# Fifteen 128-wide products in place of eighteen in the second feed-forward matmul of five of eight blocks (RWKV-6 attention, then a tanh-shrink feed-forward)

## The chip, the core and the metric

The kernel runs on one core of one Trainium2 chip. A core has TensorE (PE; its weight loads are listed apart as PEld), VectorE (DVE), ScalarE (ACT), GpSimd (POOL) and SyncE (SP, which here only issues DMAs). The metric is the device time of one execution in microseconds, as the median over runs. A profiled execution gives its own time, its span (first to last instruction) and a trace of every instruction.

## The reference

All values are 32-bit floats. Attention runs over 4 batches, 8 heads, 768 tokens and a head size of 48, and its output becomes the 3072 x 384 input of a feed-forward block of width 2048.

```python
# attention: batch 4, heads 8, seq 768, head_dim 48; w in 0.80 to 0.95
for t in range(S):
    cur = einsum('bhd,bhe->bhde', u[None] * kt, vt)
    y[:, :, t] = einsum('bhd,bhde->bhe', rt, state + cur)
    state = wt[:, :, :, None] * state + einsum('bhd,bhe->bhde', kt, vt)
x = y.transpose(0, 2, 1, 3).reshape(3072, 384)
# feed-forward: w_in 384 x 2048, w_out 2048 x 384
h = x @ w_in
g = h - tanh(h)
out = g @ w_out
```

## The kernel before

The 3072 tokens are cut into 8 blocks of 384 (4 batches, two halves each). For each block the attention result is brought into three tiles `xT` of 128 x 384 (features x tokens). The feed-forward part of a block is a loop over 16 steps `f`, one for every 128 of the 2048 hidden features. In a step, PE makes `hp`, the 128 x 384 tile of `h`, with three matmuls (`first`, L629); ACT copies it to `h` with a scale (L632); `slight` gives `g`, which for the small `h` of this data is a polynomial: DVE makes `s = h*h` and records its largest value in `top` (L643), ACT makes `qa = (s + c)^2` (L645), and DVE makes `hs = h*TOP*s` and `gT = (qa + REST)*hs` (both L635). Four steps later (`LAG`) `Second.add` multiplies it with the weights: three matmuls (L676), one for each 128 tokens, with a 128 x 128 part of `gT` as the loaded operand and 384 columns of `w_out` as the moving one, accumulated over the 16 steps into three banks of PSUM. After the last step ACT copies each bank to `o` (L681) and SP stores it.

A matmul of 32-bit floats is two records of PE and two of PEld in the trace: three matmuls show as "x6".

The attention of block i+1 is made during the steps of block i. `plan(i)` says at which step which part of it is issued: DVE and ACT preparations (`before`, `ahead`), DMA loads (`loads`) and the phases of PE: `turn` (12 transposes, L386, copied out by ACT, L388), `own` and `earlier` (two products of scores each, L363, copied under a mask by DVE, L370), `update` (L405, then eleven or so short DVE steps L417 and L428 from state to state) and `result 1` and `result 2` (L469, L486, copied out by ACT, L519, with small DMAs that fill gaps in `xT`). All phases pass through a pool of two PSUM buffers (`scratch`, the tile `att`). Each of these is written and then read in the same step. The order of work on PE, ACT, DVE and SP is that in which the code issues it; each engine works through its list in that order and waits where an operand is not there. In a step of the main loop DVE's list is: `s` of this step, `hs` and `gT` of the step before, then what `plan` asks for.

In block 0 the weights are still being loaded and converted (L205 to L213, ACT and DVE). Block 7 has no attention beside it. After the last step a sum over recorded values decides whether the whole is done again in a general way (`anew`); with this data it is not.

The change touches `slight`, `Second`, `plan`, `phase`, `update_1`, `update_2`, `before`, `inverse`, and the main loop from L798.

Of the kernel before, what the change touches and what calls it, by code (L numbers as in the profile page):

```python
# [73 lines left out]
LAG = 4  # L74
# [14 lines left out]
LEAST = 2.0 ** -24  # L89

# [6 lines left out]
def kernel(  # L97
# [16 lines left out]
    gpool = ctx.enter_context(tc.tile_pool(name="gpool", bufs=LAG + 1))  # L114
    dense = ctx.enter_context(tc.tile_pool(name="dense", bufs=3))
    conv = ctx.enter_context(tc.tile_pool(name="conv", bufs=RAWS))

    shift = const.tile([P, 5], F32, name="shift", tag="shift")
    for i, value in enumerate((QUAD[0][0], QUAD[1][0], -SMALL, -1.0, SHIFT)):
        nc.vector.memset(shift[:, i:i + 1], value)  # L120
# [7 lines left out]
    seed = const.tile([P, WIDE], BF16, name="seed", tag="seed")  # L128
# [4 lines left out]
    start = const.tile([P, WIDE], F32, name="start", tag="start")  # L133
# [49 lines left out]

    blocks_n = B * NQ
    n_whole, n_excess, n_top = blocks_n * NPAIR * NCH, 2 * blocks_n, blocks_n * NF
    holds = const.tile([P, n_whole + n_excess + n_top], F32, name="holds", tag="holds")
    excess = const.tile([P, n_excess], F32, name="excess", tag="excess")
# [34 lines left out]
    class Block:  # L224
# [7 lines left out]
        def __init__(self, b, q):  # L232
            self.b, self.q = b, q
            self.cols = slice(q * NB, (q + 1) * NB)
            self.tiles = {}
            self.ks = {}
            self.kv = {}
            self.tots = {}
# [48 lines left out]
        def before(self, p0, n):  # L287
            cols = slice(p0 * NCH * LP, (p0 + n) * NCH * LP)
            return nc.vector.tensor_tensor_scan(out=self.tile("pre")[:, cols], data0=self.tile("w")[:, cols],  # L289
                                                data1=start[:, cols], initial=0.0, op0=ALU.mult, op1=ALU.add)  # L290

        def behind(self, p0, n):
# [4 lines left out]
            def back(x):  # L297
# [4 lines left out]
                data1=back(seed[:, a:a + width]), initial=1.0, op0=ALU.mult, op1=ALU.max)  # L302
# [15 lines left out]
        def inverse(self, p0, n):  # L318
            t = self.half("post", p0, n * NCH * LP).rearrange("d (c j) -> d c j", j=LP)[:, :, 1]
            tot = self.whole(p0, n)  # L320
            nc.vector.tensor_single_scalar(tot, t, LEAST, op=ALU.max)
            to = start[:, p0 * NCH * LP:(p0 + n) * NCH * LP].rearrange("d (c j) -> d c j", j=LP)[:, :, 0]
            nc.vector.reciprocal(out=to, in_=tot)
# [57 lines left out]
        def turn(self, ps, p0):  # L381
            ks = work.tile([P, UP, NCP, P], F32, name="ks", tag="ks")
# [6 lines left out]
            self.ks[p0] = ks  # L389

        def update_1(self, ps):
            last = self.q == NQ - 1
            for cs in ((0, 1), (2,)):
                kvp = self.kv[cs[0]] = scratch(ps)
                for p in reversed(range(NPAIR)):
                    ks = self.ks[p // UP * UP]
                    for c in cs:
                        for h in range(2):
                            for par in range(2):
                                if last and 2 * c + par == NCH - 1:  # L400
# [5 lines left out]
                                                 lhsT=ks[toks, p % UP, c, 64 * h:64 * h + 64],  # L406
                                                 rhs=self.v[toks, c, e0:e0 + D], start=True, stop=True)

        def update_2(self):
# [11 lines left out]
            for c in range(NCH - 1 if self.q == NQ - 1 else NCH):  # L421
                dst = St[:, :, c + 1, 0:D] if c + 1 < NCH else states[self.q + 1][:, :, 0, 0:D]
                n0 = c // 2 % 2 * NPAIR * D
                kv = self.kv[c // 4 * 2][:, c % 2, n0:n0 + NPAIR * D].rearrange("d (p e) -> d p e", e=D)
# [7 lines left out]
        def update_any(self, ps, p0, tot):  # L432
            ks, last = self.ks[p0], self.q == NQ - 1
# [76 lines left out]
        def result_out(self, pairs, apart=False, engines=None):  # L510
            copies = []
            for p in reversed(pairs):
# [4 lines left out]
                for rows in (slice(0, D), slice(64, 64 + D)) if apart else (slice(0, P),):  # L517
                    copy = engines[len(copies) % len(engines)] if engines else nc.scalar.copy
                    copies.append(copy(out=dst[rows], in_=src[rows]))  # L519
# [9 lines left out]
        def phase(self, ps, name):  # L529
            if name == "own":  # L530
                for p0 in HALVES:
                    self.own(ps, p0)()
            elif name == "earlier":
                for p0 in HALVES:
                    self.earlier(ps, p0)()
            elif name == "turn":
                for p0 in HALVES:
                    self.turn(ps, p0)
            elif name == "update":
                self.update_1(ps)  # L540
                self.update_2()
# [3 lines left out]
            elif name == "result 2":  # L545
                self.result("from_scores", ALL, True)
                self.result_out(ALL)
                self.fill_holes([nc.sync])

# [364 lines left out]
```

## Time and profile before

| what | value |
|---|---|
| median of 4 runs | 613.83 us (613.27 to 615.51) |
| profiled execution, its own time | 613.58 us |
| its span | 611.8 us |
| mean granted clock of TensorE | 0.991 |
| first step of block 0 begins at | 28.20 us |
| first step of block 1, of block 2 | 103.74 us, 175.85 us |
| each of blocks 1 to 6, first step to first step | 72.10 us |
| block 7, 16 steps without attention | 61.9 us (3.87 us a step) |
| last matmul of `hp` ends, last `o` copied | 596.5 us, 607.6 us |

The beginnings of steps are those of the first matmul on L629. "Busy" on PE counts the time in which at least one record is open; a record of 128 x 384 lasts 486 ns and the next one starts 322 ns after it, so the duration of a record is not what it costs in a row of them. The time of one more is the distance between starts.

### The profile page before, as it was taken

What the parts mean: (1) busy time and instruction counts of PE and PEld (TensorE: products, weight loads), DVE (VectorE), ACT (ScalarE), POOL (GpSimd) and SP (SyncE); (2) the same over time, 40 slices, a digit from 0 to 9 for tenths busy, and PEclk for the clock granted to TensorE, in tenths of its full rate; (3) what the DMA queues carried; (4) which work ended last, traced back from release to release, by engine and by line L of the source; (5) the groups of instructions that cost most, each with busy time, mean ns of one, the idle gap of its engine ahead of it and who ended that gap; (6) DMA issues with size and microseconds to landing.
All of it is one profiled execution on the core that took longest, in us unless ns stands there. A gap on an engine that the chain in (4) does not pass through costs nothing.

```text
span 611.8 us, 12671 instructions
## 1 busy us (share of the span) xinstructions
PE 583.8 (95%) x5410; PEld 361.1 (59%) x5410; DVE 378.1 (62%) x777; ACT 237.4 (39%) x444; POOL 11.4 (2%) x39
## 2 busy tenths in 40 slices
PE   3669899999999999999999999999999999999996
PEld 2536566666656665566655666566665666555553
DVE  8898996855376645766367563776447663444442
ACT  4879773423325322243323333252232532223222
POOL 6000000000000000000000000000000000000000
PEclk9789999999999999999999999999999999999999
DMA  8485442203202032111211122020321100001001
GB/s 329 160 338 190 159 156 64 76 3 106 63 1 78 2 106 61 40 40 53 64 52 39 41 86 83 0 78 2 105 62 40 40 2 5 8 0 39 1 0 42
DMA packets 23420, 43.03 MB, mean 70 GB/s; under 512 B 2112, under 2 KB 21312, under 8 KB 23360
## 3 DMA queue, kind: packets, MB, share of 16 engines
q1 hardware_dynamic: 22944, 41.89, 20.5%
q8 instruction: 43, 0.70, 0.5%
q10 hardware_dynamic: 352, 0.25, 0.1%
q14 instruction: 17, 0.14, 0.1%
q0 software_dynamic: 64, 0.05, 0.0%
HBM read 36.28 MB, written 4.72 MB: 67 GB/s over the span
## 4 chain that ended last, share of the span: by engine, by line
PE 88%; DVE 6%; ACT 3%; POOL 1%; issue 1%; ACTq 0%; DVEq 0%; POOLq 0%
PE acc L676 39%; PE hp L629 38%; PE att L363 3%; PE att L469 2%; PE att L405 2%; PE att L486 2%; PE att L386 1%; DVE w_sb L213 1%; POOL mask_all L144 1%; DVE post L300 1%; DVE scores L370 1%; DVE pre L289 1%; DVE gT L635 1%; DVE w_sb L212 1%; DVE s L643 0%
## 5 line engine op out<-in xcount | busy, mean ns | idle before, releaser
L629 PE MATMUL hp<-xT,w_sb 128*128 128x384 f32 x768 | 272.7, 492 | 7.1 <-DVE w_sb L213 3.0
L676 PE MATMUL acc<-w_sb,gT 128*128 128x384 f32 x768 | 271.1, 490 | 0.8
L629 PEld LDWEIGHTS hp<-xT,w_sb 128*128 128x128 f32 x768 | 145.9, 191 | 110.9 <-ACT h L632 5.9
L676 PEld LDWEIGHTS acc<-w_sb,gT 128*128 128x128 f32 x768 | 143.0, 190 | 95.3 <-issue 1.7
L643 DVE CUSTOM_DVE_ANT_0 s<-h 128x384 f32<-128x384 f32 x128 | 71.2, 556 | 196.4 <-ACT h L632 196.2
L632 ACT ACTIVATE h<-hp 128x384 f32<-128x384 f32 x128 | 62.8, 490 | 323.1 <-PE hp L629 323.1
L635 DVE SCALAR_TENSOR_TENSOR gT<-qa,hs 128x384 f32<-128x384 f32 x128 | 71.4, 558 | 16.7 <-PE acc L676 0.5
L645 ACT ACTIVATE qa<-s,shift 128x384 f32<-128x384 f32 x128 | 77.7, 607 | 0.1
L635 DVE SCALAR_TENSOR_TENSOR hs<-h,s 128x384 f32<-128x384 f32 x128 | 70.8, 553 | 0.0
L370 DVE COPY_PREDICATED scores<-mask_all,att 128x768 f32<-128x768 uint8 x32 | 30.6, 1004 | 0.1
L300 DVE TENSOR_TENSOR_SCAN post<-w,seed 128x780 f32<-128x780 f32 x16 | 28.5, 1781 | 0.0
L289 DVE TENSOR_TENSOR_SCAN pre<-w,start 128x780 f32<-128x780 f32 x16 | 28.5, 1779 | 0.0
L386 PE MATMUL att<-ident,post 128*128 128x128 f32 x96 | 12.7, 283 | 10.1 <-DVE post L314 10.1
L328 ACT ACTIVATE k<-k,u_sb 128x384 f32<-128x384 f32 x32 | 17.7, 602 | 7.2 <-DVE post L314 7.2
L386 PEld LDWEIGHTS att<-ident,post 128*128 128x128 f32 x96 | 11.4, 146 | 12.4 <-DVE post L314 10.1
L208 ACT ACTIVATE up<-raw 128x768 f16<-128x768 f32 x16 | 17.0, 1065 | 0.0
L209 ACT ACTIVATE up<-raw 128x768 uint16<-128x768 uint32 x16 | 16.8, 1051 | 0.0
L213 DVE CUSTOM_DVE_ANT_0 w_sb<-w_sb,up 128x1536 uint16<-128x1536 uint16 (+1 forms) x17 | 15.5, 911 | 1.3 <-DVE w_sb L212 0.6
L405 PEld LDWEIGHTS att<-v_sb,ks 64*64 64x64 f32 x704 | 12.0, 135 | 6.8 <-DVE scores L370 3.6
L519 ACT COPY late<-att 128x384 f32<-128x384 f32 (+1 forms) x9 | 4.3, 478 | 29.6 <-PE att L486 28.4
L405 PE MATMUL att<-v_sb,ks 64*64 64x48 f32 x704 | 13.1, 220 | 2.7 <-DVE scores L370 2.7
L428 DVE TENSOR_TENSOR states<-states,att 128x192 f32<-128x192 f32 x40 | 14.1, 354 | 2.2
(52 smaller groups left out, 260.8 us busy)
## 6 DMA issues: line engine op xcount, KB each, us to landing
raw<-in_weights SPq DMA_DIRECT2D x16, 768.0 KB, 5.0
w<-in_wT SPq DMA_DIRECT2D x7, 780.0 KB, 4.9
k<-in_kT SPq DMA_DIRECT2D x7, 768.0 KB, 4.4
r<-in_rT SPq DMA_DIRECT2D x7, 768.0 KB, 4.7
v_sb<-in_v SPq DMA_DIRECT2D x8, 576.0 KB, 3.9
out_y<-o SPq DMA_DIRECT2D x23, 192.0 KB, 2.0
xT<-late SPq DMA_DIRECT2D x44, 24.0 KB, 1.9
w<-in_wT SPq DMA_DIRECT2D x2, 390.0 KB, 5.2
```

The lines of the kernel that those rows point to most:

```text
L213: lambda: nc.vector.tensor_tensor(out=a[:, at], in0=a[:, at], in1=up[:, at], op=ALU.add)]
L289: return nc.vector.tensor_tensor_scan(out=self.tile("pre")[:, cols], data0=self.tile("w")[:, cols], data1=start[:, cols], initial=0.0, op0 ...
L300: return nc.vector.tensor_tensor_scan(out=back(t[:, 0:width]), data0=back(self.tile("w")[:, a:a + width]), data1=back(seed[:, a:a + width] ...
L370: return lambda: nc.vector.copy_predicated(out=A[:, :, p0:p0 + UP].rearrange("s h p c t -> s h (p c) t"), mask=mask.to_broadcast([P, 2, UP ...
L386: nc.tensor.transpose(tp[:, p, c * P:(c + 1) * P], self.chunk("post", p0 + p, 2 * c, n=2), ident)
L405: nc.tensor.matmul(kvp[64 * h:64 * h + 64, par, n0:n0 + D], lhsT=ks[toks, p % UP, c, 64 * h:64 * h + 64], rhs=self.v[toks, c, e0:e0 + D], ...
L629: nc.tensor.matmul(hp, lhsT=w_in_sb[:, f, kc, :], rhs=xT[kc], start=(kc == KC - 1), stop=(kc == 0))
L632: return h, nc.scalar.activation(out=h, in_=hp, func=AF.Copy, scale=1.0 / UPSCALE)
L635: return lambda: nc.vector.scalar_tensor_tensor(out=out, in0=in0, scalar=scalar, in1=in1, op0=op0, op1=ALU.mult)
L643: nc.vector.tensor_tensor_reduce(out=s, in0=h, in1=h, scale=1.0, scalar=0.0, op0=ALU.mult, op1=ALU.max, accum_out=top[:, n:n + 1])
L645: return g, [lambda: nc.scalar.activation(out=qa, in_=s, func=AF.Square, bias=shift[:, 4:5]), product(hs, h, TOP, s, ALU.mult), product(g, ...
L676: nc.tensor.matmul(acc, lhsT=g[:, j * P:(j + 1) * P], rhs=w_out_sb[:, f, :], start=(f == 0), stop=(f == NF - 1))
```

## The change

In blocks 2 to 6 (`fast`) the steps are taken in pairs. A pair holds two 128-feature tiles of `g` for three groups of 128 tokens (six 128 x 128 parts, "0a" to "2b"), and two by three 128 x 128 parts of `w_out` ("a0" to "b2"). Their 3 x 2 by 2 x 3 product takes 18 products of 128 x 128 parts; before, these were six matmuls with 384 columns each. The change uses a bilinear scheme with 15: ten sums and differences of parts of `g` (`G_FORMS`), ten of parts of `w_out` (`W_FORMS`), fifteen products of one by one, each a matmul with 128 columns, and after the block 12 instructions that put the 15 accumulated tiles together (`SUMS`).

- PE: 15 matmuls of 128 columns for each pair, in place of 6 of 384. Twelve go into the three accumulation banks, six at `now + 2` and six at `now + 3`, counted from the pair's odd step; the other three go through a `scratch` buffer, for four pairs at a time: at step 9 (pairs 0 to 3), and at steps 0 (pairs 4 to 6) and 1 (pair 7) of the next block.
- DVE: five instructions of 128 x 256 for each pair make the forms of `g`: one after the even step, four after the odd one. `s` is no longer made on DVE in these blocks. The forms of `w_out` are made once, in steps 4 to 13 of block 1, by 20 instructions of 128 x 512. The 12 `SUMS` run at steps 4 and 5 of the next block, one instruction more (`others_summed`) before them.
- ACT, in these blocks: `s = Square(h)`, `qa`, and a `Relu(s - SLIGHT)` whose accumulated sum goes to `excess`, in this order straight after `h`; before, only `h` and `qa`. At the end four copies out of PSUM (`out`).
- `h` is multiplied in place (`hs` goes away) and has three buffers for four; `LAG` is 3 for 4.
- `plan`: block 0 `turn` 4, `own` 7, `update` 9, `earlier` 11, `result 1` 13; the others `own` 4, `earlier` 6, `turn` 8, `update` 10, `result 1` 12. `own`, `earlier` and `update` hand their DVE part back, and it is issued in the following step behind `gT` (`behind`). One of the two scans of `before`, and the reciprocals, move too.
- The end: the check is summed earlier, and the last tile of rows is copied out in halves by ACT and DVE.

```diff
-LAG = 4
+LAG = 3
+PRODUCTS = ((4, 0), (5, 2), (6, 7), (7, 8), (8, "a2"), (9, 9), (2, 3), (3, 5), ("0a", "a0"),
+            ("2a", "a1"), (0, 4), (1, 6), ("0b", "b0"), ("1b", 1), ("2b", "b1"))
+AHEAD_N, MAIN = 6, 12
+    sums = const.tile([P, 16, P], F32, name="sums", tag="sums")
+    def g_at(q, x):
+        if not isinstance(x, str):
+            return 6 + q % 2 * 4 + x if x < 4 else 10 + x
+        return (q % 2 * 3 if x[1] == "a" else 20 + q % 4 * 3) + int(x[0])
+    fast = range(2, blocks_n - 1)
...
-    def slight(h, n):
+    def slight(h, n, i, f):
...
+        if i in fast:
+            at = 2 * blocks_n + fast.index(i) * NF + f
+            q, j = divmod(f, 2)
+            g = G[:, g_at(q, "0" + "ab"[j]):g_at(q, "2" + "ab"[j]) + 1].rearrange("p t c -> p (t c)")
+            nc.scalar.activation(out=s, in_=h, func=AF.Square)
+            nc.scalar.activation(out=qa, in_=s, func=AF.Square, bias=shift[:, 4:5])
+            junk = work.tile([P, UP * NCH * LP], BF16, name="junk", tag="junk", bufs=1)
+            nc.scalar.activation(out=junk[:, 0:NB], in_=s, func=AF.Relu, bias=shift[:, 5:6],
+                                 accum_out=excess[:, at:at + 1])
...
+        return g, first + [product(h, h, TOP, s, ALU.mult), product(g, qa, REST, h, ALU.add)]
+    def form_g(q, n):
+        op, (a0, b0), (a1, b1) = G_FORMS[n][0], G_FORMS[n][1:], G_FORMS[n + 1][1:]
+        to = g_at(q, n)
+        return lambda: nc.vector.tensor_tensor(out=G[:, to:to + 2], in0=two(G, g_at(q, a0), g_at(q, a1)),
+                                               in1=two(G, g_at(q, b0), g_at(q, b1)), op=OPS[op])
+    class Fewer:
+        def product(self, to, q, n, start, stop):
+            a, b = PRODUCTS[n]
...
+            nc.tensor.matmul(to, lhsT=G[:, g_at(q, a), :], rhs=rhs, start=start, stop=stop, skip_group_check=True)
+        def add(self, q, part):
+            end = q == NF // 2 - 1
+            for n in (range(AHEAD_N), range(AHEAD_N, MAIN))[part]:
+                self.product(self.acc[:, n // 4, n % 4 * P:(n % 4 + 1) * P], q, n, q == 0 and n % 4 == 0, end)
+            if end:
+                for bank in ((0,), (1, 2))[part]:
+                    self.out(4 * bank, 4, self.acc[:, bank])
+        def others(self, ps, qs):
+            if qs[0] % 4 == 0:
+                self.apart = scratch(ps)[:, 0]
...
+        def sum(self, n, m):
+            for op, *each in SUMS[n:m]:
...
+                nc.vector.tensor_tensor(out=at[0], in0=at[1], in1=at[2], op=OPS[op])
     def plan(i):
-        ahead = {13: ("behind 2", "inverse 2"), 14: ("behind 0", "inverse 0")}
+        ahead = {13: ("behind 2", "take_whole 2"), 14: ("behind 0", "take_whole 0"), 15: ("before 2",)}
...
-            phases = {5: "turn", 8: "own", 9: "update", 11: "earlier", 13: "result 1"}
+            phases = {4: "turn", 7: "own", 9: "update", 11: "earlier", 13: "result 1"}
...
-            phases = {4: "turn", 5: "own", 6: "update", 8: "earlier", 10: "result 1"}
-            before = {0: ("before 2",), 1: ("before 0",), 2: ("times_behind 2", "times_behind 0"),
-                      3: ("times_before", "held", "times_u 2"), 4: ("times_u 0",), 7: ("bound 2", "bound 0")}
+            phases = {4: "own", 6: "earlier", 8: "turn", 10: "update", 12: "result 1"}
+            before = {0: ("before 0",), 1: ("times_behind 2",), 2: ("times_behind 0", "times_u 2"),
+                      3: ("times_before", "held", "times_u 0"), 7: ("bound 2", "bound 0")}
...
         for f in range(NF):
+            now = i * NF + f
             h, made = first(here, f, ps_d)
-            g, later_ops = slight(h, i * NF + f)
-            for op in rest + extra:
+            g, later_ops = slight(h, now, i, f)
+            for op in rest + behind + extra:
                 op()
-            rest = later_ops
+            rest, behind = later_ops, []
...
+            if i in fast:
+                q = f // 2
+                rest += [form_g(q, n) for n in (range(2, len(G_FORMS), 2) if f % 2 else (0,))]
+                if f % 2:
+                    due += [(now + 2, second.add, (q, 0)), (now + 3, second.add, (q, 1))]
+                if f == 9:
+                    second.others(ps_a, range(4))
+            else:
+                due.append((now + LAG, second.add, (f, g)))
...
+            if i == 1 and fast and 4 <= f < 14:
+                for q in (0, 4):
+                    form_w(f - 4, q)
+            if f in (4, 5) and summed:
+                summed[0].sum(*((0, 6) if f == 4 else (6, len(SUMS))))
...
+            if f < 2 and summed:
+                summed[0].others(ps_a, ((4, 5, 6), (7,))[f])
+                if f:
+                    behind.append(summed[0].others_summed)
+            while due and due[0][0] <= now:
+                _, add, what = due.pop(0)
+                add(*what)
```

## The prediction, made before the changed kernel was run

> **What bounds it now.** I read the page's first two parts, then the windows of one block, the timeline of its steps, and the groups by shape. From the page:
>
> ```profile
> span 611.8 us, 12671 instructions
> PE 583.8 (95%) x5410; PEld 361.1 (59%) x5410; DVE 378.1 (62%) x777; ACT 237.4 (39%) x444; POOL 11.4 (2%) x39
> ```
>
> One block (4) in the windows view; columns are the stretch, its length, then busy us (and instructions) of PE, PEld, DVE, ACT, POOL, then clock, DMA share, GB/s:
>
> ```profile
> 320.00:392.10 72.10, 71.99 (x669) 44.70 (x668) 43.91 (x91) 24.03 (x49) 0.13 (x2) 1.00 0.17 53
> ```
>
> PE is never free in a block, DVE is free for 28 us of 72 and ACT for 48. So PE's own work sets the time, and the steps show what it consists of (timeline: start, length, engine, line):
>
> ```profile
> 333.59 2.10 PE L676 MATMUL acc<-w_sb,gT 128*128 128x384 f32 x6
> ...
> 335.53 2.10 PE L629 MATMUL hp<-xT,w_sb 128*128 128x384 f32 x6
> ...
> 337.46 1.47 PE L386 MATMUL att<-ident,post 128*128 128x128 f32 x12
> ...
> 338.77 2.10 PE L676 MATMUL acc<-w_sb,gT 128*128 128x384 f32 x6
> ...
> 340.71 2.10 PE L629 MATMUL hp<-xT,w_sb 128*128 128x384 f32 x6
> ...
> 342.74 1.63 PE L363 MATMUL att<-r,k 48*64 48x64 f32 x96
> ```
>
> Three matmuls take 335.53 - 333.59 = 1.94 us (1.935 over many), 322 ns a record, 0.84 ns a column. A plain step is 3.87 us, and the phases add 72.10 - 16 x 3.87 = 10.2 us to a block.
>
> **Term 1, the products.** A pair of steps has 12 records of L676 now: 12 x 0.3225 = 3.87 us. After, it has 30 records with 128 columns. The trace has no such product; three rows bound it. The transposes are 128 columns behind a 128-column load: (1.47 - 0.273, the last record's length) / 11 = 109 ns a record. Their load is short, though:
>
> ```profile
> L386 PEld LDWEIGHTS att<-ident,post x96: 138/141/231, 10.1 to 482.8; 128*128 128x128 f32 x96
> ```
> ```profile
> L676 PEld LDWEIGHTS acc<-w_sb,gT x768: 186/190/192, 46.4 to 606.2; 128*128 128x128 f32 x192
> ```
> ```profile
> L363 PEld LDWEIGHTS att<-r,k x768: 129/135/228, 11.6 to 488.3; 48*64 48x64 f32 x192
> ```
>
> A true load of 128 columns lasts 190 ns, one of 64 columns 135: 55 ns for 64 columns, so 128 columns occupy 110 ns and 80 is latency. L363 has load and matmul equally wide (64), and keeps up: (1.63 - 0.218) / 95 = 14.9 ns a record, four of which run side by side, 59 ns for 64 columns. Doubled, that is 119 ns. So 109 (transposes) to 119 (L363 doubled); I take 110, nearest to the row of the same width and to the load's own 110. A pair then takes 3.30 us, saves 0.57, and 40 pairs save **22.8 us** (24.0 at 109; 12.0 at 119).
>
> The Trainium skill speaks against this ("TensorE: Matmul & The Clock Gate", Back-to-back issue gap): in streams of load and matmul, 128 columns take about 81 ns where the isolated gap would be 56. If that ratio held here (128 columns at 0.84 ns are 107 ns; x 1.45 = 155 ns), a pair would take 4.65 us and the term would be an estimated +31 us. The L363 row (load and matmul equally wide, 59 ns against 53 of columns) shows no such ratio, so I set it aside.
>
> **Term 2, DVE in blocks 2 to 6.** Its durations, from the timeline of the same block:
>
> ```profile
> 323.19 0.55 DVE L635 SCALAR_TENSOR_TENSOR hs<-h,s 128x384 f32<-128x384 f32 x1
> ...
> 323.88 0.56 DVE L635 SCALAR_TENSOR_TENSOR gT<-qa,hs 128x384 f32<-128x384 f32 x1
> ...
> 324.35 1.77 DVE L289 TENSOR_TENSOR_SCAN pre<-w,start 128x780 f32<-128x780 f32 x1
> ...
> 351.07 0.35 DVE L428 TENSOR_TENSOR states<-states,att 128x192 f32<-128x192 f32 x1
> 351.46 0.36 DVE L417 TENSOR_TENSOR states<-states,whole 128x192 f32<-128x192 f32 x1
> ```
>
> `hs` to `gT` takes 0.69 us, `gT` to an independent next 0.47; an instruction of 192 columns that needs the one before follows after 0.39. A column costs about 1.04 ns (L307: 1536 columns 1.75 us, L314: 768 columns 0.95), so a dependent 256-column one is 0.39 + 64 x 1.04 ns = 0.46 us. The forms are mostly a chain. After an even step DVE has 0.69 + 0.6 + one form = 1.65 us, after an odd one 0.69 + 0.6 + 4 x 0.46 = 3.1 (with waits on PE for the buffers). Per block: 8 x 4.75 = 38; scans 4 x 1.7, with their small ones 8; masks 4 x 0.9; state steps 11 x 0.39 = 4.3; L314 and L307 3.5; `SUMS` 12 x 0.42 = 5; `others_summed` 0.5. Together 63 us, where PE needs 72.1 - 8 x 0.57 = 67.5. It fits, barely, so order decides.
>
> PE's step is now 1.94 + 6 products x 0.22 = 3.25; with phases (own and earlier 1.75 each, turn 1.3, update 1.75, results 3.6) and `others`, steps 0 to 6 are 5.2, 3.9, 3.25, 3.25, 5.0, 3.25, 5.0. DVE's lists from step 14 on: 5.0 (odd rest, scan), 3.6, then in the next block 5.1, 2.5, 4.5, 3.4, 5.5 (odd rest, 6 sums), 6.0 (even rest, own, 6 sums), 3.1: 38.7 us with no gap. It can start when ACT has `s` of step 13, 1.2 us after that `hp`. PE comes to the first product of step 7 38.6 us after the same `hp`. So forms of pair 2 end at 39.9, where PE wants its first at 38.6 and its last 0.9 later: some 0.5 us late, and then the two buffers of `earlier`, which `turn` at step 8 takes over, come some 0.5 us late too. What is late next is only the rest of that block: from step 9 DVE's lists are shorter than PE's steps. Blocks 3 to 6 have it (block 2 has no sums before it). I take 1.5 us each, **+6**: the sum leaves no slack, and waits on PE for the form buffers cost more than I counted. Bounds: if the 25 small instructions in that stretch run at the independent distance (0.34), nothing is late, 0; if each takes 0.6, 25 x 0.14 = 3.5 us more, +20 in four blocks.
>
> **Term 3, ACT.** `h`, `s`, `qa` each wait for the one before: 0.53 + 0.64 + 0.51, then the Relu with its read of the sum (L334: 0.93 for 780 columns; 384 columns as L645's distance 0.51, and 0.22 for the read): 2.4 us of a 3.25 us step. It is over in step 2, with `times_u` (1.0, two of L328) and two copies of 512 columns from PSUM (0.5 each): 4.5 us. `h` of step 3 is then some 1.2 us late; PE has one buffer for `hp` and 1.3 us of products meanwhile, copy included 0.4 us short: **+1.5** over four blocks; 0 (where term 2's waits cover it) to 3. Elsewhere (step 7 with `bound` 2.1 more, step 9, step 12) the next PE step holds a phase that covers it; without that cover step 7 would cost 0.5.
>
> **Term 4, block 1.** Twenty forms of `w_out`, 128 x 512: 0.95 - 0.27 = 0.6 us apart, 12 us, in a block where DVE was free for 28: hidden; uncovered, +12. The state steps, though, now run in step 11 behind `s` and `gT`: from the end of `hp` 0.5 + 0.5 + 1.2 + 3.9 = 6.1 us, while `result 1` wants the last states 3.87 + 1 = 4.9 us after it: **+1.2** (0 to 3, with the mask steps beside the forms).
>
> **Term 5, ends and block 0.** One product step more in block 0's first four, where PE waits (3.0 us for `w_sb`), one less in the tail; DVE's masks two steps ahead of `update`, where PE waited 1.5 us; the check's 0.5 us wait before the last products gone; half copies at the end 0.2. DVE is 95% busy in block 0, so most of this comes back elsewhere: **-2** (-4 to +2). The moved loads (`w`, `k`, `r` at 8, 9, 11) keep their steps, the six stores a block leave SP at step 5 with nothing behind them before step 8, and `xT`'s gap DMAs leave at step 12 with 10 us to block end: nothing, covered by those steps; late they would hold the next block's first `hp` by their own 3 us.
>
> **Sum.** Against the profiled execution's own 613.58 us (span 611.8; the runs' median is 613.83): -22.8 + 6 + 1.5 + 1.2 - 2 = -16.1, **597.5 us**.
>
> **Rivals.** (a) *DVE becomes the bound of the fast blocks*: 52 small instructions a block; at 0.6 us each DVE needs 63 + 52 x 0.14 = 70 us, which leaves 2 us a block: -10 in five, +1, with ends about 604. For: 63 of 67.5 already. Against: the 0.39 row of dependent ones is firm. (b) *All is hidden*: 613.6 - 24.0 - 2 = 588. For: ACT and DVE have slack from step 9 on. Against: the tally above. (c) **Slower**: the weight load does not go under a narrow matmul, so that each record waits for its own load, 190 ns. Place: every product; price 30 x 190 = 5.7 us a pair, +1.83 x 40 = +73, 685 us. It decides from (3.87 - 6.7/40)/30 = 123 ns a record, where the gain is gone. For: in L676 a load of 190 has 322 ns to hide in, no row shows a full-array 190 behind 109. Against: L363 at 59 ns, with loads of 135. (d) *It doesn't do what it says*: the check fails and all is made anew, at eight more blocks of at least 72 us over 1150 us; the new `excess` sums ask the same of `h` as `top` did.
>
> **Chances.** Forecast (592 to 602) 0.47, (a) 0.20, (b) 0.18, (c) and milder forms of it, or of (a) past 0.68 us an instruction, 0.11, (d) 0.01, near no change 0.03. A measurement tells some 0.3% (2 us) from no change. Faster 0.85, same 0.03, slower 0.12. The range runs from all hidden (588) to (a) with records a little over 110 ns (608).
>
> **What would show it.** Records of the products 110 ns apart (over 119: term 1 wrong; over 123: slower). Fast blocks 67 to 70 us from first step to first step, the first of them shortest; PE waiting for the forms at step 7 and for DVE's masks at step 8; DVE about 90% busy; block 1 near 73. If PE waits for ACT more than for DVE, term 3 is mis-sized; if no wait shows at all, terms 2 and 3 are.

## The result, and the profile after

The changed kernel takes 615.52 us (median; 610.17 to 620.38) where the kernel before, beside it on the same chip, takes 614.27 us (612.99 to 617.01). The ratio is 1.0011 [1.0000, 1.0021]: no change that can be told. It goes by the fast runs alone (the two slowest after, 619.74 and 620.38 us, are left out as slow), so it is not the quotient of the two medians. The forecast was 597.5 us, its range 588 to 608. The profiled execution took 613.53 us with a span of 611.8 us, the same span as before. From the page of the kernel after, the span, the busy times of the engines and the granted clock in 40 slices:

```profile
span 611.8 us, 14793 instructions
...
PE 570.6 (93%) x6130; PEld 407.1 (67%) x6130; DVE 456.2 (75%) x906; ACT 339.8 (56%) x689; POOL 9.9 (2%) x39
...
PEclk9899999899999899999999999999999999999999
```

PE is busy for 13 us less, and the span is no shorter: PE has idle time that it did not have. One late block (4) in the windows view (stretch, length, busy us and instructions of PE, PEld, DVE, ACT, POOL, then clock, DMA share, GB/s):

```profile
325.99:395.27 69.28, 68.09 (x814) 53.32 (x813) 57.02 (x113) 44.37 (x99) 0.13 (x2) 1.00 0.19 55
```

Such a block did gain: 69.28 us for 72.10. So the loss is elsewhere, and the starts of the first `hp` of each block say where:

| block | 0 | 1 | 2 | 3 to 6, each | 7 and the end | span |
|---|---|---|---|---|---|---|
| before, us | 75.54 | 72.11 | 72.09 | 72.10 | 75.5 | 611.8 |
| after, us | 75.49 | 79.12 | 74.03 | 69.3 | 77.9 | 611.8 |
| difference | 0 | +7.0 | +1.9 | -2.8 | +2.4 | 0 |

Blocks 3 to 6 win 11.2 us; blocks 1 and 2 and the end lose 11.4. Block 1 has none of the 15-product scheme on PE. In the timeline of its step 2 (start, length, engine, line; in brackets the idle time before, and who ended it):

```profile
113.24 0.81 PE L739 MATMUL acc<-w_sb,sums 128*128 128x384 f32 x2
...
115.34 0.47 ACT L754 ACTIVATE o<-acc 128x384 f32<-128x384 f32 x1
...
115.87 0.91 PE L739 MATMUL acc<-w_sb,sums 128*128 128x384 f32 x2 [1.82 <-ACT o L754]
...
116.82 0.49 ACT L754 ACTIVATE o<-acc 128x384 f32<-128x384 f32 x1 [1.00 <-PE acc L739]
...
117.36 1.65 PE L739 MATMUL acc<-w_sb,sums 128*128 128x384 f32 x2 [0.58 <-ACT o L754]
...
118.80 3.05 PE L668 MATMUL hp<-xT,w_sb 128*128 128x384 f32 x6
```

These are the last matmuls into block 0's three banks and the copies out of them. PE ends bank 0, then waits 1.82 us until ACT has copied bank 0 before it starts on bank 1, and again 0.58 us before bank 2. In the kernel before, the same six records stand as one group of 2.10 us. The last two lines show a second price: the six `hp` records behind the wait last 3.05 us, not 2.10; the clock in the window from 113.50 to 121.70 is 0.79. The same place in block 2 is worse, since ACT's list has more ahead of the copy (`s`, `qa`, the Relu and `times_u` of that step):

```profile
192.35 0.81 PE L739 MATMUL acc<-w_sb,sums 128*128 128x384 f32 x2
196.28 1.65 PE L739 MATMUL acc<-w_sb,sums 128*128 128x384 f32 x2 [3.12 <-ACT o L754]
198.51 1.65 PE L739 MATMUL acc<-w_sb,sums 128*128 128x384 f32 x2 [0.58 <-ACT o L754]
199.95 3.43 PE L668 MATMUL hp<-xT,w_sb 128*128 128x384 f32 x6
```

In the waits view of the kernel after (engine and line, waited for: us in total, times, longest us) this is the largest wait of PE that is new, with the same thing in the fast blocks behind it (L782 is the copy of the accumulated tiles there):

```profile
PEld acc L739 <- ACT o L754: 11.5, 6, 3.7
DVE o L749 <- DMA out_y<-o: 8.1, 1, 8.1
PE acc L739 <- ACT o L754: 7.3, 6, 3.1
PEld acc L771 <- ACT sums L782: 6.8, 4, 1.7
```

One line of the diff could explain such a wait: the three accumulation tiles `acc0` to `acc2` have become one tile `acc` of three banks. If the program tracks its operands by tiles, a write to a tile waits for every earlier read of it, so that a matmul into bank 1 waits for the copy out of bank 0. That is the theory of the experiments. Its rivals are that the fast blocks' new work on ACT or DVE holds PE back, and that the phases handed to the next step do.

Block 1 has another new wait, at `result 1`, which reads the last `states`. Engines and lines as above:

```profile
161.15 2.10 PE L668 MATMUL hp<-xT,w_sb 128*128 128x384 f32 x6
164.02 0.33 PE L510 MATMUL att<-pre,states 48*64 48x64 f32 x4 [0.78 <-DVE states L469]
165.65 1.56 PE L510 MATMUL att<-pre,states 48*64 48x64 f32 x90 [1.30 <-DVE states L469]
```

That step, 12, takes 9.82 us from `hp` to `hp`; without the wait it takes 7.38 us (`split_now` below).

### The profile page after: what moved, and what is told of

The parts are those of the page before. It is cut to its first block, busy times and chain, and to the rows that moved or that the text cites. A ratio compares the mean times of both kernels' runs of the same rounds, so it can differ in the third digit from the quotient of the medians.

```text
span 611.8 us, 14793 instructions
## 1 busy us (share of the span) xinstructions
PE 570.6 (93%) x6130; PEld 407.1 (67%) x6130; DVE 456.2 (75%) x906; ACT 339.8 (56%) x689; POOL 9.9 (2%) x39
## 4 chain that ended last, share of the span: by engine, by line
PE 82%; ACT 8%; DVE 2%; issue 2%; DMA 0%; DVEq 0%; ACTq 0%
PE hp L668 37%; PE acc L771 17%; PE acc L739 14%; PE att L771 4%; PE att L399 4%; PE att L510 2%; PE att L447 2%; PE att L527 2%; PE att L422 1%; ACT up L246 1%; ACT k L364 1%; ACT h L671 1%; ACT up L247 1%; ACT w_sb L243 1%; ACT sums L782 1%
## 5 line engine op out<-in xcount | busy, mean ns | idle before, releaser
L771 PE MATMUL acc<-forms,g 128*128 128x128 f32 x720 | 108.9, 278 | 4.9 <-ACT sums L782 4.3
L771 PEld LDWEIGHTS acc<-forms,g 128*128 128x128 f32 x720 | 95.9, 191 | 18.5 <-ACT sums L782 6.8
L712 DVE TENSOR_TENSOR g<-g 128x256 f32<-128x256 f32 x200 | 85.0, 425 | 19.9 <-PE acc L771 1.6
L674 DVE SCALAR_TENSOR_TENSOR h<-h,s 128x384 f32<-128x384 f32 x128 | 70.6, 551 | 33.5 <-ACT s L686 33.5
L739 PE MATMUL acc<-w_sb,sums 128*128 128x384 f32 x192 | 71.3, 505 | 6.3 <-ACT o L754 6.1
L695 DVE CUSTOM_DVE_ANT_0 s<-h 128x384 f32<-128x384 f32 x48 | 26.7, 555 | 56.7 <-ACT h L671 56.7
L674 DVE SCALAR_TENSOR_TENSOR g<-qa,h 128x384 f32<-128x384 f32 x96 | 53.6, 558 | 18.4 <-PE acc L771 7.4
L689 ACT ACTIVATE junk<-s,shift 128x384 bf16<-128x384 f32 x80 | 47.9, 599 | 0.0
L686 ACT ACTIVATE s<-h 128x384 f32<-128x384 f32 x80 | 41.9, 524 | 2.5
L771 PEld LDWEIGHTS acc<-w_sb,g 128*128 128x128 f32 x240 | 33.2, 192 | 0.0
L406 DVE COPY_PREDICATED scores<-mask_all,att 128x768 f32<-128x768 uint8 x32 | 30.7, 1010 | 0.9 <-PE att L399 0.9
L739 PEld LDWEIGHTS acc<-w_sb,g 128*128 128x128 f32 x96 | 18.0, 190 | 14.3 <-ACT o L754 2.4
```

Of the source, the lines that this page charges most:

```text
L406: return lambda: nc.vector.copy_predicated(out=A[:, :, p0:p0 + UP].rearrange("s h p c t -> s h (p c) t"), mask=mask.to_broadcast([P, 2, UP ...
L674: return lambda: nc.vector.scalar_tensor_tensor(out=out, in0=in0, scalar=scalar, in1=in1, op0=op0, op1=ALU.mult)
L686: nc.scalar.activation(out=s, in_=h, func=AF.Square)
L689: nc.scalar.activation(out=junk[:, 0:NB], in_=s, func=AF.Relu, bias=shift[:, 5:6], accum_out=excess[:, at:at + 1])
L712: return lambda: nc.vector.tensor_tensor(out=G[:, to:to + 2], in0=two(G, g_at(q, a0), g_at(q, a1)), in1=two(G, g_at(q, b0), g_at(q, b1)), ...
L739: nc.tensor.matmul(acc, lhsT=g[:, j * P:(j + 1) * P], rhs=w_out_sb[:, f, :], start=(f == 0), stop=(f == NF - 1))
```

## The experiments

Ratios are against the kernel before, run beside each kernel. Unless said otherwise, the diffs are against the kernel after; `...` stands for lines left out. Every kernel here computes the whole output. Steps and blocks are read from the one profiled execution of each kernel, medians from all its runs.

### Three accumulation tiles again (split)

```diff
-                acc = self.acc[:, j, 0:DM]
+                acc = self.acc[j][:, 0:DM]
...
-                self.product(self.acc[:, n // 4, n % 4 * P:(n % 4 + 1) * P], q, n, q == 0 and n % 4 == 0, end)
+                self.product(self.acc[n // 4][:, n % 4 * P:(n % 4 + 1) * P], q, n, q == 0 and n % 4 == 0, end)
...
-                    self.out(4 * bank, 4, self.acc[:, bank])
+                    self.out(4 * bank, 4, self.acc[bank])
...
-    acc = ps_d.tile([P, NB // P, BANK], F32, name="acc", tag="acc")
+    acc = [ps_d.tile([P, BANK], F32, name=f"acc{j}", tag=f"acc{j}") for j in range(NB // P)]
```

> The changed kernel with its three accumulation banks as three tiles in place of one tile of three banks; nothing else. Theory A (a matmul into one bank of the one tile waits for ScalarE's copies out of its other banks): the waits at step 2 of blocks 1 and 2 (steps of 7.5 and 9.5 us for 3.9), at steps 3 of blocks 3 to 6 (4.6 for 3.3) and in the tail (two of 1.2 us) go, together about 17 us with the half clock that follows them: near 598 us. Rival B (the copies are late because of ScalarE's own list, and the banks really are needed): no change, 613 to 616 us.

605.30 us (603.30 to 605.51), ratio 0.9842 [0.9820, 0.9865]. The one line of the diff costs 10 us, in the direction expected but short of the size: part of what was won at one place came back at others. Block 2 falls from 74.03 to 68.90 us. Block 1 falls only from 79.12 to 76.22: step 2 is plain again, but its wait at `result 1` is now followed by records at half clock, and step 12 takes 11.39 us for 9.82. Blocks 3 to 6 stay at 69.0 to 69.4 us: step 3, where PE waited for ACT, takes 3.56 us for 4.62 (3.27 without any wait), but in its place PE waits for DVE. Timeline of steps 7 and 8 of block 4:

```profile
348.79 0.95 DVE L712 TENSOR_TENSOR g<-g 128x256 f32<-128x256 f32 x2
349.80 0.57 PEld L771 LDWEIGHTS acc<-forms,g 128*128 128x128 f32 x4 [0.30 <-DVE g L712]
...
350.69 0.52 PEld L771 LDWEIGHTS acc<-forms,g 128*128 128x128 f32 x4 [0.32 <-DVE g L712]
...
352.77 1.93 DVE L406 COPY_PREDICATED scores<-mask_all,att 128x768 f32<-128x768 uint8 x2
...
353.89 0.64 PEld L422 LDWEIGHTS att<-ident,post 128*128 128x128 f32 x6 [0.65 <-PE hp L668]
...
354.81 0.64 PEld L422 LDWEIGHTS att<-ident,post 128*128 128x128 f32 x6 [0.28 <-PE att L422]
```

PE's loads wait for the forms of `g` (L712) at step 7. At step 8 the two halves of `turn` (L422) start each just behind one of the two masked copies (L406, the second ends at 354.70), which free their buffers; that the copies are what they wait for is read from these times, as the profile names other engines. These are the two places that the prediction named for its Term 2; in the kernel after, the wait on ACT at step 3 covers them.

### The single tile put into the kernel before (before_tile)

```diff
-                self.acc = [self.ps.tile([P, DM], F32, name=f"acc{j}", tag=f"acc{j}", bufs=1)
-                            for j in range(NB // P)]
-            for j, acc in enumerate(self.acc):
+                self.acc = acc_all
+            for j in range(NB // P):
+                acc = self.acc[:, j, 0:DM]
...
+    acc_all = ps_d.tile([P, NB // P, BANK], F32, name="acc", tag="acc")
```

> The kernel before, its three accumulation tiles made one tile of three banks, nothing else. Theory A (matmuls into one bank wait for ScalarE's copies out of the others): at each of seven block changes the last product step waits for two copies, as at step 2 of block 1 in the changed kernel (4.6 us with the half clock behind it), and the tail 2.5: near 645 us. If the wait in the changed kernel came from ScalarE's longer list instead, this one stays at 614.

637.09 us (635.34 to 641.00), ratio 1.0393 [1.0359, 1.0426]; the diff is against the kernel before, and nothing else of the change is in it. Timeline of this kernel at the place shown above:

```profile
119.48 0.47 ACT L681 ACTIVATE o<-acc 128x384 f32<-128x384 f32 x1
120.00 0.91 PE L676 MATMUL acc<-w_sb,gT 128*128 128x384 f32 x2 [1.82 <-ACT o L681]
120.95 0.49 ACT L681 ACTIVATE o<-acc 128x384 f32<-128x384 f32 x1 [1.00 <-PE acc L676]
121.50 0.91 PE L676 MATMUL acc<-w_sb,gT 128*128 128x384 f32 x2 [0.58 <-ACT o L681]
```

The same two waits, to the hundredth. That step takes 6.81 us for 3.87, 2.94 us more, in each of six blocks (75.04 us for 72.10); block 7 and the end take 79.4 for 75.5. 6 x 2.94 + 3.9 is 21.5 of the 21.7 us by which the span grew. So the single tile costs some 22 us where all blocks use the plain product. It is less than expected; the records behind these waits ran at full speed.

### The copies behind the matmuls, with the single tile (order)

```diff
                 nc.tensor.matmul(acc, lhsT=g[:, j * P:(j + 1) * P], rhs=w_out_sb[:, f, :],
                                  start=(f == 0), stop=(f == NF - 1))
+            for j in range(NB // P):
+                acc = self.acc[:, j, 0:DM]
                 if f == NF - 1:
```

> The changed kernel with its one accumulation tile, but in a slow block's last product step the three copies are issued behind all nine matmul records' groups, not each behind its own. Theory A (the tile is what is waited for, in the order of issue): no copy stands between the banks, the long steps 3 of block 1 and block 2 shorten to 3.9 and about 5, the copies run beside the next hp; the tail gets some 1 us longer: 605 to 609 us. Rival (matmuls and copies cannot use neighbouring banks at one time): no change, 613 to 616.

609.84 us (606.92 to 611.78), ratio 0.9916 [0.9883, 0.9948], just outside what was expected. The six records of the closing step stand together again. What is left is that the next block's first write waits for all three copies: timeline of step 3 of block 1 in this kernel:

```profile
113.55 2.10 PE L739 MATMUL acc<-w_sb,sums 128*128 128x384 f32 x6
115.49 2.10 PE L668 MATMUL hp<-xT,w_sb 128*128 128x384 f32 x6
118.75 2.20 PE L739 MATMUL acc<-w_sb,sums 128*128 128x384 f32 x6 [1.16 <-ACT o L756]
```

Step 3 of block 1 takes 5.30 us, where 3.9 was expected, and blocks 3 to 6 keep their 4.62 us at step 3; block 1 is no shorter (79.09 us), since step 12 now takes 12.94 us. So the order in the code inside one tile makes the wait, as the theory says, and other tiles remove it, while another order only makes it smaller. The rival of neighbouring banks is out: with three tiles, matmuls into one bank run beside copies out of the others (`split`, block 4, under Term 3 below).

### Without the 15 products, single tile and three tiles (nofast, nofast_split)

```diff
-    fast = range(2, blocks_n - 1)
+    fast = range(2, 2)
...
-            g = ring(sums, 0, n) if i < 2 else ring(G, 20, n)
+            g = ring(sums, 0, n) if i < 2 or not fast else ring(G, 20, n)
```

> The changed kernel without the 15 products (no block is in the fast set; one accumulation tile as in the change), so all that the change does around them. Theory A: each of seven block changes costs about 4.5 us as at the start of block 1, the state steps make result 1 wait 2.4 us in blocks 1 to 6, the tail 2.5: near 660 us. Rival B: what was lost is lost in the fast blocks by ScalarE and VectorE, and this one stands within 3 us of the kernel before, 614.

> As the one before it, with three accumulation tiles. Theory A: only the 2.4 us wait for the states in blocks 1 to 6 is left, and some 2 us won at both ends: near 626 us. If instead the forms of w_out in block 1 make that wait, they are not there now, and it is 610 to 613 us.

`nofast`: 671.24 us (666.73 to 674.05), ratio 1.0923 [1.0871, 1.0975]. `nofast_split`: 640.41 us (639.91 to 641.58), ratio 1.0418 [1.0395, 1.0441]. `nofast_split` has the three tiles besides. The tile makes 31 us between the two, where 34 were expected, but they are 11 and 14 us above what was expected. With this new plan and none of the fast products the kernel is slower than before by 26 us even with three tiles; so what costs time is not only in the tile, and not in the forms of `w_out` either, which neither kernel makes. The timeline of `nofast_split` shows the place, step 12 of block 1:

```profile
159.84 0.33 PE L510 MATMUL att<-pre,states 48*64 48x64 f32 x4 [0.78 <-DVE states L469]
161.47 2.71 PE L510 MATMUL att<-pre,states 48*64 48x64 f32 x92 [1.30 <-DVE states L469]
164.27 4.20 PE L739 MATMUL acc<-w_sb,sums 128*128 128x384 f32 x6
```

The waits of 0.78 and 1.30 us are those of the kernel after; here six records take 4.20 us behind them (640 ns each from start to start, for 322). Step 12 takes 9.83 to 12.97 us in every block, where 7.38 is plain. The short expectation had priced the wait without the slower clock behind it.

### The DVE part of the phases at once (split_now, nofast_split_now)

```diff
-                    behind += later.phase(ps_a, phases[f])
+                    handed = later.phase(ps_a, phases[f])
+                    if i == 1:
+                        for op in handed:
+                            op()
+                    else:
+                        behind += handed
```

Both kernels have the three tiles. In `nofast_split_now` the condition is `if i:`, and it has the two lines of `nofast`.

> Three accumulation tiles, and in block 1 the VectorE part of a phase is issued in the phase's own step again (masks in steps 4 and 6, state steps in step 10). Theory: result 1 at step 12 of block 1 waits because the state steps stand a step later behind s and gT: its step goes from 11.4 us to 7.4, 601 to 602 us. Rival (the forms of w_out crowd VectorE in block 1, whatever the order): the step stays above 9 us, 604 to 606 us.

> No block in the fast set, three accumulation tiles, and from block 1 on the VectorE part of a phase in its own step: what is left of the change is the places of the phases, LAG 3, h in place and the ends. Theory: the 26 us that the run without it lost against the kernel before all come from the state steps handed to the next step; 611 to 614 us. If the places of the phases cost something themselves, more.

`nofast_split_now`: 615.31 us (612.92 to 616.02), ratio 1.0011 [0.9997, 1.0024], blocks of 72.20 us; 1.3 us above what was expected. With three tiles and the state steps at once, the new plan with the plain products is as fast as the kernel before. These two edits account for all that the change costs in blocks without fast products.

`split_now`: 603.37 us (599.16 to 605.86), ratio 0.9801 [0.9774, 0.9829]. Step 12 of block 1 is at 7.38 us for 11.39 and the block at 72.21 for 76.22. The total gained less than these 4 us, and less than expected: in the profiled executions block 2 went from 68.90 to 73.53 us. Its steps 3 and 4 took 7.0 and 7.8 us behind a wait that the next kernel shows; in `split` that wait is 1.79 us long, here 3.79.

### Scans further ahead (split_now_scans)

```diff
+        if i >= 2:
+            ahead = {11: ("behind 2", "take_whole 2"), 12: ("behind 0", "take_whole 0"), 13: ("before 2",), 14: ("before 0",)}
+            if i >= 3:
+                before.pop(0)
```

> As split_now, and from block 2 on the four scans with their small ones at steps 11 to 14 of the block, for 13, 14, 15 and 0 of the next. Theory (the prediction's tally: VectorE's lists from step 14 to step 8 are what makes steps 5, 8 and 9 of blocks 3 to 6 late): these waits, 0.9 us a block, go, and blocks 3 to 6 take 68.2 us for 69.3: some 4 us under split_now, 597 to 598. If the 69.3 us come from PE's own work, no change.

601.46 us (600.26 to 602.43), ratio 0.9791 [0.9770, 0.9813]; some 4 us above what was expected. The edit is added to `split_now`, and takes about a step of work out of DVE's lists before step 7. Blocks 3 to 6 did what was expected: 68.3 us each, 0.6 to 1.1 less than in `split_now`. So DVE's order does cost those blocks some 0.9 us each once the tile no longer covers it. The total does not show it: the median is 1.9 us lower, less than the runs of `split_now` differ among themselves. Block 2 again took long, 73.60 us. The timeline of this kernel at step 3 of block 2:

```profile
188.05 0.84 ACT L754 ACTIVATE o<-acc 128x384 f32<-128x384 f32 x2
...
192.82 0.49 ACT L754 ACTIVATE o<-acc 128x384 f32<-128x384 f32 x1 [3.93 <-DMA out_y<-o]
193.21 0.48 ACT L671 ACTIVATE h<-hp 128x384 f32<-128x384 f32 x1
...
193.75 4.21 PE L668 MATMUL hp<-xT,w_sb 128*128 128x384 f32 x6 [3.57 <-ACT h L671]
```

`o` has two buffers. The third copy waits 3.93 us for the store of the first, on ACT's list, with `h` of the next step behind it; PE has one buffer for `hp`, stands for 3.57 us, and resumes at half clock.

### A buffer of its own for the third copy (split_obufs, best)

```diff
-                            o = dense.tile([P, DM], F32, name="o", tag="o", bufs=2)[:, at]
+                            o = dense.tile([P, DM], F32, name="o", tag="s" if engine is nc.scalar else "qa")[:, at]
-                    o = dense.tile([P, DM], F32, name="o", tag="o", bufs=2)
+                    o = dense.tile([P, DM], F32, name="o", **(dict(tag="qa") if j == 2 else dict(tag="o", bufs=2)))
```

> Three accumulation tiles and the separate buffer for the third copy, nothing else. Theory: 1.4 us from step 4 of block 2 and 2 us from the tail under the run with three tiles: 601 to 603 us. Rival: no change, 605.

> Three accumulation tiles, block 1's VectorE parts in their own step, the scans at steps 11 to 14, and the third copy of a slow block's rows in a buffer of its own (that of qa, and s at the very end), so that no copy waits for a DMA to leave. Theory: in block 2 ScalarE stands 3.9 us at the third copy with h of step 3 behind it, so steps 4 and 5 (7.2 and 7.7 us) become 3.6 and 5.1; the tail loses some 2 us of such waits: 593 to 595 us. Rival (ScalarE's own work is too long there): steps 4 and 5 keep 10 us or more, 599 to 601.

Added to `split`: 601.83 us (599.70 to 602.37), ratio 0.9785 [0.9752, 0.9818]. Added to `split_now_scans` (`best`): 593.06 us (592.44 to 593.99), ratio 0.9650 [0.9625, 0.9675]. Both are within what was expected. In `best`, block 2 takes 67.20 us, blocks 3 to 6 take 68.3, block 1 takes 72.11, and the end 75.0. From the page of `best`, the busy times, PE with 96% of the span for 93%:

```profile
PE 565.4 (96%) x6130; PEld 406.9 (69%) x6130; DVE 456.1 (77%) x906; ACT 338.7 (57%) x689; POOL 9.9 (2%) x39
```

The timeline of `best` at the place of the last experiment: three copies together, and `h` at once behind them:

```profile
189.03 1.22 ACT L754 ACTIVATE o<-acc 128x384 f32<-128x384 f32 x3
...
190.14 0.49 ACT L671 ACTIVATE h<-hp 128x384 f32<-128x384 f32 x1
```

And the windows view of `best` over 68 us from block 4 into block 5, in which PE is free for 0.2 us:

```profile
313.00:381.00 68.00, 67.77 (x812) 53.35 (x811) 56.55 (x112) 44.24 (x98) 0.13 (x2) 1.00 0.19 56
```

This version beats both kernels; it takes 3.5% less than the one before.

### `h` squared on DVE, with three tiles (split_sdve)

```diff
-            nc.scalar.activation(out=s, in_=h, func=AF.Square)
-            nc.scalar.activation(out=qa, in_=s, func=AF.Square, bias=shift[:, 4:5])
-            junk = work.tile([P, UP * NCH * LP], BF16, name="junk", tag="junk", bufs=1)
-            nc.scalar.activation(out=junk[:, 0:NB], in_=s, func=AF.Relu, bias=shift[:, 5:6],
-                                 accum_out=excess[:, at:at + 1])
-            first = []
...
+        nc.vector.tensor_tensor_reduce(out=s, in0=h, in1=h, scale=1.0, scalar=0.0, op0=ALU.mult,
+                                       op1=ALU.max, accum_out=top[:, n:n + 1])
+        first = [lambda: nc.scalar.activation(out=qa, in_=s, func=AF.Square, bias=shift[:, 4:5])]
```

> Three accumulation tiles, and h squared on VectorE again in all blocks (with its maximum into top; no Square and no Relu on ScalarE in blocks 2 to 6). If VectorE's list is as full as the prediction's tally (63 us of 67.9 a block), 8 us more a block make it the bound: some 3 to 5 us a block slower than the run with three tiles, 612 to 622 us. If the tally was too high (no wait for VectorE is seen in the changed kernel), within 3 us of the run with three tiles, 596 to 601 us.

671.72 us (669.34 to 676.20), ratio 1.0955 [1.0916, 1.0993]: a miss by some 50 us. It undoes the part of the change that moves `s` to ACT; with it `qa` goes back behind the next step's `h` on ACT's list, and the Relu falls away. Sixteen more instructions of 0.56 us a block would be 9 us of DVE where 12 are free, and a little late was expected. But blocks 3 to 6 take 81 to 86 us. Step 6, in which PE now waits for the masked copies, takes 7.1 to 10.9 us for 5.03, and step 12, in which it waits for the states, 11.8 to 13.7 for 6.79; the clock over the span falls to 0.956. From the waits view of this kernel:

```profile
PE att L510 <- DVE states L469: 18.0, 12, 3.0
PE att L399 <- DVE scores L406: 11.5, 5, 3.3
PE acc L763 <- DVE g L704: 10.7, 11, 1.7
```

All three are waits for DVE. So with this order of the lists the scheme needs `h` squared on ScalarE, and the margin on DVE cannot be read off its busy share; whether another order would make room for it was not tried. How the 66 us over `split` divide between waits and clock was not taken apart.

## Why the prediction was wrong, point by point

**The step that failed** is the accounting of the change's parts outside the fast products. Term 3 took the copies out of PSUM as work of ACT and nothing more, Term 5 took the ends as "half copies at the end 0.2", and no term holds the three banks becoming one tile, although the diff has it in every line with `self.acc[:, ...]`. What this left out is read from the kernel after against `best`, in which these waits are gone but for 0.3 us in each of blocks 3 to 6:

- Block 1 takes 79.12 us for 72.11: 4.6 at the tile (steps 2 and 3 take 7.49 and 4.82 for 3.87 each) and 2.4 at `result 1`.
- Block 2 takes 74.03 us for 67.20, at the tile (steps 2 and 3 take 9.53 and 4.60 for 3.87 and 3.44).
- Blocks 3 to 6 take 69.3 us for 68.3 each (step 3 takes 4.62 for 3.56).
- The end takes 77.9 us for 75.0: 1.6 at the tile (the copies of the three banks start 1.49 us apart, for 0.65 and 0.70) and 0.9 at the store of `o` (below, Term 5).

That is 20.5 us, as much as the 20.8 us that the products win (Term 1). Some 17 of it stand at the single tile, which the prediction put at nothing. `split`, `before_tile` and `order` show this cause. `split`, with the tile alone undone, gained 10.2 us and not 17, since a wait for DVE took its place in blocks 3 to 6, the wait at `result 1` cost 1.6 us more and the wait for a store came into block 2; at 605.30 us it already lies inside the range of the forecast. `best` is 4.4 us below the forecast.

**Term 1** was right and slightly mis-sized. Eight products' records take 1.05 us, the last of them 0.275: (1.05 - 0.275) / 7 = 111 ns, and two fast steps without a phase take 6.55 us, of which 3.87 are `hp` and 24 records are the rest: 111.7 ns. A pair takes 30 x 111.7 ns = 3.35 us, saves 0.52, and 40 pairs save 20.8 us, not 22.8. Rival (c), the load that is not hidden, is out: it would have needed more than 123 ns a record, and 190 were its price. The Trainium skill ("TensorE: Matmul & The Clock Gate", Back-to-back issue gap) has about 81 ns for a matmul of 128 columns in a stream of loads and matmuls, where the isolated gap is about 56, that is 1.45 times. Here it is 111.7 ns for 107.5 of columns, 1.04 times, so that ratio, which the prediction set aside, does not hold for this case.

**Term 2** was right in its places and near in its size: 1.5 us a block was predicted, 0.9 measured, as the difference between `split_now` and `split_now_scans` in blocks 3 to 6. But in the kernel after its +6 us are not there, since the wait for the single tile comes first. The forms take what was worked out: 425 ns busy on average for 128 x 256, 0.46 us from one to the next that needs it. DVE's busy share in such a block is 57.0 of 69.3 us, 82%, not the 90% of the tally.

**Term 3** named the right engine, the right step and about the right symptom: PE waits for ACT at step 3, and the step is 1.35 us longer, not 0.4. The reason was another. Timeline of ACT in the kernel after, in block 4:

```profile
335.62 0.57 ACT L782 ACTIVATE sums<-acc 128x512 f32<-128x512 f32 x1
...
340.57 1.05 ACT L782 ACTIVATE sums<-acc 128x512 f32<-128x512 f32 x2
```

And of PE there:

```profile
341.68 1.16 PE L771 MATMUL acc<-forms,g 128*128 128x128 f32 x8 [1.08 <-ACT sums L782]
```

The products at 341.68 write bank 0 first, which ACT had copied at 336.2; they wait for the copies of banks 1 and 2. With three tiles (`split`) the same products start at 332.96, beside the copies of banks 1 and 2 (333.09 to 334.14). What is left is a wait of 0.31 us for `h`, as predicted and close to the 0.4.

**Term 4** was right in its mechanism (state steps handed to step 11, late for `result 1`) and half the size: 2.4 us measured, 1.2 predicted, and up to 5.6 us where the clock falls behind it. `split_now` removes it, and the 20 forms of `w_out` are hidden, as said: block 1 then takes 72.21 us with them.

**Term 5** had -2 us and got none of it. Block 0 did not change (75.49 for 75.54). Its DVE is also less full than the term says: busy for 67.65 of 75.54 us, 90%; 95% is its share from 60 to 80 us alone. The end is 2.4 us longer, of which 0.9 are products of block 6 in the first three steps of block 7 (12.50 us for 11.61). The wait for the check before the last products, which was to be gone, is 0.77 us for 0.48. The last copy waits for a store, since `o` has two buffers (timeline of the kernel after):

```profile
606.79 0.36 DVE L749 TENSOR_SCALAR o<-acc 128x192 f32<-128x192 f32 x1 [8.09 <-DMA out_y<-o]
```

ACT's half of the same bank, at 605.56, began 1.23 us sooner; in `best` 0.37 us lie between the two. The buffer of its own in `best` takes this away, and with it the wait in block 2.

**The rivals.** (a) did not happen: DVE is not the bound. (b), all hidden at 588, did not happen either; `best`, at 593.06 between (b) and the forecast, needed four edits that the change does not have. What did happen, near no change, had 0.03. Of the signs to watch, the records came as said (111.7 ns), and blocks 3 to 6 lie in the 67 to 70 us. But block 2, which was to be the shortest of the five with the 15 products, took 74.03 us, block 1 took 79.12 and not about 73, and the waits at steps 7 and 8 show only with three tiles. The sentence "If PE waits for ACT more than for DVE, term 3 is mis-sized" was the one that applied.

## What to carry to other kernels

When a diff merges accumulators or buffers into one tile, look at every reader of it: a write to one part may wait for the read of another part, and the price is one wait at each change of block, also in the blocks that the change does not mean to touch. Count the buffers between a copy and its store for all the copies that can be under way, because a copy that waits on an in-order engine holds up everything behind it. A saving on the bounding engine counts only after every new wait has been priced; the small ones here were together as large as the whole gain.

## What the hardware showed that was not expected

A short wait of PE can cost more than its length. After the kernel's waits of 1.82 and 0.58 us in block 1, and of 3.12 us in block 2, the next records stand 640 ns apart instead of 322; windows view of the kernel after around the two places:

```profile
113.50:121.70 8.20, 5.80 (x13) 2.73 (x12) 2.46 (x5) 3.30 (x7) 0.00 (x0) 0.79 0.20 73
...
192.30:203.30 11.00, 7.30 (x14) 3.40 (x13) 7.03 (x13) 4.59 (x10) 0.00 (x0) 0.69 0.17 60
```

The third column from the right is the granted clock, 0.79 and 0.69 for 1.00. The same waits of 1.82 and 0.58 us in `before_tile` were followed by records at full speed, and 2.1 us at `result 1` cost 2.4 us in one kernel and 5.6 in another. The runs spread with it: the run of the kernel after that took 610.17 us has a granted clock of 0.989 over its span, the one that took 618.40 us has 0.976. The Trainium skill ("TensorE: Matmul & The Clock Gate", What's actually happening) has the clock halve after an idle window of about 3.4 us that runs freely of the kernel. That identical waits end differently agrees with a free-running window. That the window need not be wholly idle is shown in block 1: from 113.88 to 117.29 us PE is busy for 1.08 of 3.41 us, and from 117.29 to 120.70 the clock is 0.50.
